# Three real products a complex one in the columns of an inverse transform, with weight preparation moved to GpSimd and its DMAs

## The chip, the cores and the metric

The kernel runs on one core of a Trainium2 chip. The metric is the device time of one execution in microseconds (us); the median of several runs is given. A core has TensorE (PE in the profile; its weight loads are PEld), VectorE (DVE), ScalarE (ACT), GpSimd (POOL), and SyncE (SP), which here only issues DMAs. Each engine works through its own instructions in order and waits on semaphores for the others. DMAs are issued from SP, ACT and POOL.

## The reference

What is computed is one block of a network on x of 2048 rows and 512 columns, in f32. Six rows of modulation (sa, ca, ga, sb, cb, gb) come from `silu(c) @ w_mod`. Then:

```python
h = _layernorm(x, axis=-1) * (1 + ca) + sa
x = x + ga * _A_ref(h, A_w_r, A_w_i)   # irfft2(rfft2(h) * (w_r + 1j * w_i))
h = _layernorm(x, axis=-1) * (1 + cb) + sb
x = x + gb * _B_ref(h, B_w1, B_b1, B_w2)   # mish(h @ w1 + b1) @ w2, 1376 wide inside
```

## The kernel before

The kernel has four stages. Stage 1 (the plan `opening`) norms x and does the forward transform: row products, then column products over 128 rows for each of 16 residues n. Stage 2 (the plan `middle`) multiplies by the spectral weights in 17 groups of columns; `store_d` writes its result into two tiles `dd[0]` and `dd[1]`, eight residues n each, in the layout [n, j, c, q]: c is the real part, the imaginary part, and minus the real part; j counts four interleaved columns, q 64 frequencies. Stage 3 finishes the inverse transform: `p3_col(n)` multiplies the complex columns of residue n by a complex matrix, `p3_row(n)` does the inverse along rows with `kiv` and adds to x. Stage 4 is the dense part: `up` products with w1, mish, `down` products with w2, over four pairs of blocks i and five groups t of 256 of the inner width (a sixth, single group is 96 wide).

The products of stage 4 work in a split f32 form: each operand is a high part, rounded to f32r, and a low part, the difference; three products (`TERMS`) stand for one. Most of stage 4 uses seven products of quarter blocks in place of eight, so sums of quarters of w1 and of w2 are prepared too. This preparation runs beside stage 3 and the first pair of stage 4:

- `load_w1(t)` brings a group of w1; `block_w1(t, a)` casts a quarter to its high part on ACT (line 872) and subtracts to get the low part on DVE (line 873); `sum_w1(t, a, step)` forms a sum on DVE (line 893) and later splits it; `keep_w1` writes the split quarters to DRAM, from where `fetch_w1` brings them again for later pairs into a ring of eight tiles `wr`.
- `load_w2(t)` brings a group of w2; `sum_w2` forms four sums on DVE (line 1046); `split_w2` casts on ACT (line 1049) and subtracts on DVE (line 1050).

In stage 3, `p3_col(n)` has for each of four j two products into one region of a bank: real and imaginary columns by `kc[0]` (line 992), imaginary and minus the real ones by `kc[1]` (line 993). A product of f32 operands 128 by 128 shows as two passes in the profile, so a residue has 16 passes there. ACT copies the whole bank out (line 995), `p3_row` makes four products from the copy (line 1002, eight passes), and DVE adds the bank to x and sums its rows (line 1005). `row_squares` then scales the sum on ACT (line 1009) and sums squares on ACT (line 1010).

Nothing but the order of emission schedules the work. Each step is put into a plan with a key; the keys sort the steps, and a list of places written out by hand, `ORDERS`, gives the order in which the sorted steps are emitted, one list for each of three plans (stages 1, 2, and 3 with 4). Since each engine runs in order, this list sets all queues, those of DMA issues too. POOL's queue holds low parts of stage 1, one product of stage 2, some of `store_d`, the issue of `send` and `turn_out` (rows turned through DRAM), and the last accumulation into x.

Of the kernel before, what the change touches and what calls it, by code (L numbers as in the profile page):

```python
# [102 lines left out]
def tile_spectral_block(ctx: ExitStack, tc: tile.TileContext, x_d, w1_d, b1_d, w2_d,  # L103
# [44 lines left out]
    def plain(t):  # L148
        return t.bitcast(F32)
# [19 lines left out]
    mraw = big.tile([P, N2, 256], F32, name="mraw", tag="da")  # L169
    mring = big.tile([P, 8, 2, 384], F32R, name="mring", tag="db")  # L170
    wmc = big.tile([P, 4, 512], F32, name="wmc", tag="cr")
    wms = big.tile([P, 4, 512], F32, name="wms", tag="ci")

    first = ExitStack()
    pw = first.enter_context(tc.tile_pool(name="pw", bufs=1))
# [1463 lines left out]
```

## Time and profile before

| | us |
|---|---|
| median of 3 runs | 368.36 (367.98 to 369.48) |
| span of the profiled execution | 365.9 |
| DVE busy | 302.7 |
| ACT busy | 266.5 |
| POOL busy | 77.5 |

The span goes from the first to the last instruction of one profiled execution; the time of a run is taken outside it, and the median stands 2.5 us above this span. Stage 1 takes the first 50 us or so, stage 2 goes to 89 us, the column products of stage 3 run from 90.4 to 131.4 us, and the first products with w1 begin at 131.8 us. In the views, a line such as L992 is a line of the kernel; "out<-in" names the tiles; "x16" counts instructions. Busy time of an engine that nobody waits for costs nothing, and a busy PE may still be waiting inside, since the ends of its matmuls are modelled; so the starts of its instructions are of more use than its busy share.

### The profile page before, as it was taken

What the parts mean: (1) busy time and instruction counts of PE and PEld (TensorE: products, weight loads), DVE (VectorE), ACT (ScalarE), POOL (GpSimd) and SP (SyncE); (2) the same over time, 40 slices, a digit from 0 to 9 for tenths busy, and PEclk for the clock granted to TensorE, in tenths of its full rate; (3) what the DMA queues carried; (4) which work ended last, traced back from release to release, by engine and by line L of the source; (5) the groups of instructions that cost most, each with busy time, mean ns of one, the idle gap of its engine ahead of it and who ended that gap; (6) DMA issues with size and microseconds to landing.
All of it is one profiled execution on the core that took longest, in us unless ns stands there. A gap on an engine that the chain in (4) does not pass through costs nothing.

```text
span 365.9 us, 7823 instructions
## 1 busy us (share of the span) xinstructions
PE 358.1 (98%) x2676; PEld 334.6 (91%) x2676; DVE 302.7 (83%) x751; ACT 266.5 (73%) x603; POOL 77.5 (21%) x126
## 2 busy tenths in 40 slices
PE   8999999999999999999999999999999999999995
PEld 7999977768999998798999999999999999999994
DVE  0899977879799889989996677997588984779995
ACT  1789879997799999998767577765686654456650
POOL 0488828787011001100002201005001000000000
PEclk9999999999999999999999999999999999999998
DMA  6999997884669869999889985778989567883133
GB/s 223 380 352 331 380 373 254 275 308 149 179 221 294 265 219 299 253 301 307 276 226 316 303 271 116 261 228 212 283 261 284 188 187 232 238 299 60 60 57 116
DMA packets 54343, 89.96 MB, mean 246 GB/s; under 512 B 7552, under 2 KB 20960, under 8 KB 54048
## 3 DMA queue, kind: packets, MB, share of 16 engines
q1 hardware_dynamic: 49728, 74.65, 62.3%
q0 software_dynamic: 2416, 7.87, 9.4%
q10 hardware_dynamic: 2160, 6.95, 5.5%
q8 instruction: 21, 0.34, 0.4%
q14 instruction: 18, 0.15, 0.1%
HBM read 68.21 MB, written 17.57 MB: 234 GB/s over the span
## 4 chain that ended last, share of the span: by engine, by line
PE 85%; DVE 5%; ACT 3%; POOL 2%; issue 1%; DMA 1%; SPq 0%; ACTq 0%; DVEq 0%; POOLq 0%
PE bank L1224 24%; PE bank L1124 22%; PE bank L1107 6%; PE bank L276 4%; PE bank L992 4%; PE bank L1002 4%; PE bank L993 4%; PE bank L324 3%; PE bank L1170 3%; PE bank L1220 3%; PE bank L325 2%; PE bank L326 2%; DMA wmc<-in_w_mod_dram 1%; PE bank L648 1%; PE bank L624 1%
## 5 line engine op out<-in xcount | busy, mean ns | idle before, releaser
L1124 PE MATMUL bank<-hT,wr 128*128 128x256 f32 x360 | 51.8, 283 | 0.0
L1124 PEld LDWEIGHTS bank<-hT,wr 128*128 128x128 f32 x360 | 47.2, 191 | 0.7
L1124 PE MATMUL bank<-hB,wr 128*128 128x256 f32 x318 | 45.4, 284 | 0.0
L1124 PEld LDWEIGHTS bank<-hB,wr 128*128 128x128 f32 x318 | 41.5, 191 | 0.7
L1276 POOL DMA_DIRECT2D x<-modr x7 | 6.3, 898 | 141.3 <-ACT ah L1049 37.8
L1224 PE MATMUL bank<-w2a,ah 128*128 128x256 f32 x161 | 34.8, 283 | 0.0
L1050 DVE TENSOR_TENSOR al<-buf,ah 128x512 fp32r<-128x512 f32 (+1 forms) x45 | 30.0, 670 | 5.0 <-ACT ah L1049 4.9
L1224 PE MATMUL bank<-w2b,ah 128*128 128x256 f32 x147 | 32.2, 283 | 0.0
L1049 ACT CAST ah<-buf 128x512 fp32r<-128x512 f32 (+1 forms) x45 | 26.8, 603 | 4.1 <-PE bank L1224 1.8
L1224 PEld LDWEIGHTS bank<-w2a,ah 128*128 128x128 f32 x161 | 27.0, 192 | 0.3
L1224 PEld LDWEIGHTS bank<-w2b,ah 128*128 128x128 f32 x147 | 25.0, 191 | 0.6
L992 PE MATMUL bank<-kc,d 128*128 128x128 f32 x128 | 24.9, 276 | 0.5 <-ACT d L545 0.5
L993 PE MATMUL bank<-kc,d 128*128 128x128 f32 x128 | 24.8, 275 | 0.0
L1107 PE MATMUL bank<-hB,wr 128*128 128x512 f32 x96 | 23.8, 391 | 0.0
L1224 PE MATMUL bank<-w,ah 128*128 128x256 f32 x112 | 21.5, 284 | 0.0
L1107 PEld LDWEIGHTS bank<-hB,wr 128*128 128x128 f32 x96 | 17.6, 188 | 3.5
L324 PE MATMUL bank<-buf,mring 128*128 128x512 f32 x48 | 20.5, 426 | 0.0
L992 PEld LDWEIGHTS bank<-kc,d 128*128 128x128 f32 x128 | 19.4, 192 | 0.7 <-ACT d L545 0.7
L993 PEld LDWEIGHTS bank<-kc,d 128*128 128x128 f32 x128 | 19.4, 192 | 0.0
L697 PEld LDWEIGHTS bank<-kv,a_sb 128*128 128x128 f32 x126 | 15.6, 192 | 3.4 <-issue 1.4
L1224 PEld LDWEIGHTS bank<-w,ah 128*128 128x128 f32 x112 | 17.6, 191 | 0.4
L921 POOL DMA_DIRECT2D turned<-x x16 | 9.3, 662 | 40.9 <-DVE buf L1194 22.4
(308 smaller groups left out, 1097.5 us busy)
## 6 DMA issues: line engine op xcount, KB each, us to landing
wr<-w_S SPq DMA_DIRECT2D x60, 256.0 KB, 3.7
wr<-w_A SPq DMA_DIRECT2D x45, 256.0 KB, 3.8
w_S<-hT SPq DMA_DIRECT2D x20, 256.0 KB, 3.0
x<-in_A_x_dram SPq DMA_DIRECT2D x16, 256.0 KB, 4.7
xring<-in_x_t_dram SPq DMA_DIRECT2D x16, 256.0 KB, 4.8
w_A<-wr SPq DMA_DIRECT2D x15, 256.0 KB, 3.9
x<-modr POOLq DMA_DIRECT2D x7, 512.0 KB, 5.4
out_dram<-x SPq DMA_DIRECT2D x7, 512.0 KB, 3.3
```

Source lines behind the costliest of these rows:

```text
L276: nc.tensor.matmul(pgv[:, j], data(j), krs[:, j, :].rearrange("p (c q) -> p c q", c=2), start=True, stop=True)
L324: nc.tensor.matmul(pa, m[:, a, 0:128], g, start=(i == 0), stop=False)
L697: nc.tensor.matmul(pd[:, i * P:(i + 1) * P], y[:, i * P:(i + 1) * P], kv[:, 0:128], start=True, stop=True)
L992: nc.tensor.matmul(o, dj[:, 0:128], kc[0][:, n, :], start=True, stop=False)
L993: nc.tensor.matmul(o, dj[:, 64:192], kc[1][:, n, :], start=False, stop=True)
L1002: nc.tensor.matmul(px[:, j * P:(j + 1) * P], e[:, j * P:(j + 1) * P], kiv[:, j, :], start=True, stop=True)
L1049: nc.scalar.copy(h, r)
L1050: nc.vector.tensor_tensor(l, r, plain(h), op=ALU.subtract)
L1107: nc.tensor.matmul(ups[i, t, f], ring[t, a][:, p, b, :], sides[int(a[2]) - 1][:, :, q, b, :], start=(a[2] == "1" and b == 0 and n == 0), s ...
L1124: nc.tensor.matmul(o, w[:, p, k, :], h[:, q, k, :], start=(first and n == 0), stop=(last and n == 5), skip_group_check=True)
L1170: nc.tensor.matmul(ups[i, 0][:FL], w1s[:, p, u, :], sides[u // 2][:, :, q, u % 2, :], start=(u == 0 and p + q == 0), stop=(u == 3 and p == ...
L1224: nc.tensor.matmul(out_ps[b][n][:, 256 * half:256 * half + 256], a[p][:, e], w2[t][q][:, r], start=(t == 1 and half == 0 and i == 0), stop ...
```

## The change

Let a column be R + iI and the matrix C + iS, as `kc` now holds them in three planes: C, S - C and -C - S. The old form took RC - IS and RS + IC by four real products. The new one takes (R + I)C, then R(S - C) and I(-C - S): the first plus the second is the imaginary part, the first plus the third the real part. `dd` gets the layout [c, n, j, q], with R + I in the third place of c, where minus R was. A residue's steps are now:

- `p3_col`: R by S - C into the first half of a bank, R + I by C into the second, two matmuls of 128 columns each (eight passes);
- `p3_copy`: ACT copies the second half out to `g2`;
- `p3_imag`: two DVE adds of bank and copy, 64 partitions each, into the imaginary half of `e`;
- `p3_last`: I by -C - S, added to the second half in the bank (four passes), from the new tiles `kch`;
- `p3_real`: two ACT copies, 64 partitions each, into the real half of `e`;
- `p3_row` as before, one residue later; banks alternate between tags A and D.

`store_d` forms R + I with an addition on DVE or POOL after the copy, in place of the scaling by -1 on ACT, DVE or POOL. The tiles `kch` (1 MB) are loaded from SP's queue in stage 2 and lie in the pool `act`, whose two buffers later hold `acts`; that pool is opened at the start now, and `acts` is one tile of both parts.

The weights: the high parts of the quarters of w1, and of the raw blocks of w2, come straight from DRAM by DMAs issued from POOL that write f32r (`high_w1`, `high_w2`); the casts on ACT for these are gone. Low parts of quarters of w1, for groups 1 and 2, and of w2, for groups 1 to 3, and the sums of the same groups, are formed on POOL and not on DVE. The casts and low parts of the sums of w1 stay on ACT and DVE. The scaling in `row_squares` goes from ACT to POOL. `single_w1` takes `wsum` and not `g2` for its raw block.

The order lists of the second and third plan are new; that of the first is the same. In stage 2 the new list differs in the last third, from about the eleventh group on. In the third plan all steps move: `p3_col` runs two to three residues ahead of `p3_row`, columns 5 and 4, and 9 and 8, change places, `row_squares` of residues 7 to 15 go behind the last columns, `high_w1` stands several steps before its `block_w1`, and the first `up` products come in between the last column steps, before `p3_last` 13.

```diff
-    dd = [big.tile([P, 8, 4, 3, NQ], F32, name=f"d{i}", tag=t) for i, t in enumerate(("da", "db"))]
+    dd = [big.tile([P, 3, 8, 4, NQ], F32, name=f"d{i}", tag=t) for i, t in enumerate(("da", "db"))]
...
-        elif kind == "all":
-            nc.scalar.mul(minus, s[:, :, 0, :], -1.0)
-        elif kind != "pool" and i:
-            nc.vector.tensor_scalar(minus, s[:, :, 0, :], -1.0, None, op0=ALU.mult)
+        elif kind == "all" or kind != "pool" and i:
+            nc.vector.tensor_tensor(both, s[:, 1], dst[:, 0, :, q0:q0 + nq], op=ALU.add)
         else:
-            nc.gpsimd.tensor_scalar(minus, dst[:, :, 0, q0:q0 + nq], -1.0, None, op0=ALU.mult)
+            nc.gpsimd.tensor_tensor(both, dst[:, 0, :, q0:q0 + nq], dst[:, 1, :, q0:q0 + nq], op=ALU.add)
...
+    def load_kch(i):
+        nc.sync.dma_start(kch[i], kc_d[:, 2, N2 // 2 * i:N2 // 2 * i + N2 // 2, :])
...
+    def high_w1(t, a):
+        slot_w1((t, a))
+        nc.gpsimd.dma_start(ring[t, a][:, 0], w1_block(t, a))
+
     def block_w1(t, a):
-        slot_w1((t, a))
-        split_w1(ring[t, a], w1_block(t, a, src[t]))
+        w = ring[t, a]
+        (nc.gpsimd if t < 3 else nc.vector).tensor_tensor(w[:, 1], w1_block(t, a, src[t]), plain(w[:, 0]), op=ALU.subtract)
...
-            nc.vector.tensor_tensor(v, p, q, op=op)
+            (nc.gpsimd if t < 3 else nc.vector).tensor_tensor(v, p, q, op=op)
...
     def p3_col(n):
-        d = dd[n // 8][:, n % 8]
-        pe = bank("A")
-        for j in range(4):
-            dj = d[:, j].rearrange("p c q -> p (c q)")
-            o = pe[:, j * P:(j + 1) * P]
-            nc.tensor.matmul(o, dj[:, 0:128], kc[0][:, n, :], start=True, stop=False)
-            nc.tensor.matmul(o, dj[:, 64:192], kc[1][:, n, :], start=False, stop=True)
-        e = buf("g1")
-        nc.scalar.copy(e, pe)
-        st["e", n] = e
+        d = dd[n // 8][:, :, n % 8].rearrange("p c j q -> p c (j q)")
+        st["pe", n] = pe = bank("AD"[n % 2])
+        for i, (c, k) in enumerate(((0, kc[1]), (2, kc[0]))):
+            for a in range(2):
+                o = pe[:, (2 * i + a) * P:(2 * i + a + 1) * P]
+                nc.tensor.matmul(o, d[:, c, P * a:P * a + P], k[:, n, :], start=(i == 0 and a == 0), stop=True,
+                                 skip_group_check=True)
+
+    def p3_copy(n):
+        st["s", n] = s = buf("g2")[:, 0:2 * P]
+        nc.scalar.copy(s, st["pe", n][:, 2 * P:])
...
+    def p3_imag(n):
+        st["e", n] = e = buf("g1")
+        to = e.rearrange("p (a b s) -> p b a s", a=2, b=2)
+        for b, (pe, s) in enumerate(zip(halves_of(st["pe", n][:, 0:2 * P]), halves_of(st.pop(("s", n))))):
+            nc.vector.tensor_tensor(to[IM, b], pe, s, op=ALU.add)
+
+    def p3_last(n):
...
+            nc.tensor.matmul(pe[:, (2 + a) * P:(3 + a) * P], d[:, 1, P * a:P * a + P], kch[n // 8][:, n % 8, :],
+                             start=False, stop=True, skip_group_check=True)
+
+    def p3_real(n, b):
+        to = st["e", n].rearrange("p (a b s) -> p b a s", a=2, b=2)
+        nc.scalar.copy(to[RE, b], halves_of(st["pe", n][:, 2 * P:])[b])
...
-        nc.scalar.mul(mv[:, n, 0:1], mv[:, n, 0:1], -D ** -1.5)
+        nc.gpsimd.tensor_scalar(mv[:, n, 0:1], mv[:, n, 0:1], -D ** -1.5, None, op0=ALU.mult)
...
-            nc.vector.tensor_tensor(tsum[:, o], a, b, op=ALU.subtract)
+            (nc.gpsimd if t < 4 else nc.vector).tensor_tensor(tsum[:, o], a, b, op=ALU.subtract)
+
+    def high_w2(t):
+        h = w2[t][0].rearrange("p e d -> p (e d)")
+        for e, f, rows in tiles(t):
+            nc.gpsimd.dma_start(h[:, 256 * e:256 + 512 * e], w2_d[f * P:f * P + rows, 0:256 + 256 * e])
+
+    def split(h, l, r, low=None, high=True):
+        if high:
+            nc.scalar.copy(h, r)
+        (low or nc.vector).tensor_tensor(l, r, plain(h), op=ALU.subtract)
...
+        low = nc.gpsimd if 0 < t < 4 else None
...
-            split(h[:, 768:], l[:, 768:], tsum.rearrange("p e d -> p (e d)"))
+            split(h[:, 768:], l[:, 768:], tsum.rearrange("p e d -> p (e d)"), low)
         else:
             u, v = st["w2", t]
-            split(h[:, 0:256], l[:, 0:256], u[:, 0:256])
-            split(h[:, 256:768], l[:, 256:768], v)
+            split(h[:, 0:256], l[:, 0:256], u[:, 0:256], low, False)
+            split(h[:, 256:768], l[:, 256:768], v, low, False)
...
-        plan.at(1.5 if last else n - N2 + 1.1, p3_row, n)
-        plan.at(1.6 if last else n - N2 + 1.3, row_squares, n)
+        plan.at(n - N2 + 0.2, p3_copy, n)
+        plan.at(n - N2 + 0.3, p3_imag, n)
+        plan.at(n - N2 + 1.02, p3_last, n)
+        for b in range(2):
+            plan.at(n - N2 + 1.04, p3_real, n, b)
+        plan.at(1.5 if last else n - N2 + 2.1, p3_row, n)
+        plan.at(1.6 if last else n - N2 + 2.3, row_squares, n)
...
-    kc = np.stack([z.real, -z.imag], 1)
+    kc = np.stack([z.real, z.imag - z.real, -z.real - z.imag], 1)
```

More of the change, by code (lines that the diff above doesn't have):

```diff
@@ L172, in tile_spectral_block @@
     wms = big.tile([P, 4, 512], F32, name="wms", tag="ci")
+    act = ctx.enter_context(tc.tile_pool(name="act", bufs=2))
+    kch = [act.tile([P, N2 // 2, P], F32, name="kch", tag="act") for _ in range(2)]
     first = ExitStack()
@@ L531, in tile_spectral_block @@
         opening.run(0)
-    dd = [big.tile([P, 8, 4, 3, NQ], F32, name=f"d{i}", tag=t) for i, t in enumerate(("da", "db"))]
+    dd = [big.tile([P, 3, 8, 4, NQ], F32, name=f"d{i}", tag=t) for i, t in enumerate(("da", "db"))]
     def store_d(g, i, part, kind):
         q0, nq = groups[g]
-        src = st["pd", g][:, 0:nq * 128].rearrange("p (q a c) -> p a c q", q=nq, c=2)
-        dst = dd[i].rearrange("p n d c q -> p (n d) c q")
-        s = src[:, 32 * i:32 * i + 32]
-        to, minus = dst[:, :, 0:2, q0:q0 + nq], dst[:, :, 2, q0:q0 + nq]
+        src = st["pd", g][:, 0:nq * 128].rearrange("p (q a c) -> p c a q", q=nq, c=2)
+        dst = dd[i].rearrange("p c n d q -> p c (n d) q")
+        s = src[:, :, 32 * i:32 * i + 32]
+        to, both = dst[:, 0:2, :, q0:q0 + nq], dst[:, 2, :, q0:q0 + nq]
         if part == 0:
@@ L826, in tile_spectral_block @@
             put(load_kc, s - 11)
+            put(load_kch, s - 11)
     with tc.manual_schedule():
@@ L901, in single_w1 @@
         if load:
-            src[0] = buf("g2")[:, 0:4 * FL].rearrange("p (k f) -> p k f", k=4)
+            src[0] = wsum[:, 0:4 * FL].rearrange("p (k f) -> p k f", k=4)
             nc.sync.dma_start(src[0], w1v[:, :, (NF - 1) * P:F])
@@ L1198, in halves @@
         if k == 0:
-            acts[b, t] = [act.tile([P, 7, P], F32R, name=n) for n in ("ah", "al")]
+            both = act.tile([P, 2, 7, P], F32R, name="act", tag="act")
+            acts[b, t] = [both[:, k] for k in range(2)]
         if k < len(parts[b, t]):
@@ L1326, in tile_spectral_block @@
             plan.at(s - N2 + 0.6, fn, *[a for a in args if a is not None])
+            if fn is load_w2:
+                plan.at(s - N2 + 0.7, high_w2, t)
     plan.at(13.6 - N2, load_w2, 0)
@@ L1354, in tile_spectral_block @@
         for a, key in zip(QUARTERS, keys):
+            plan.at(key - 1, high_w1, t, a)
             plan.at(key, block_w1, t, a)
@@ L1462, in tile_spectral_block @@
     plan.at(12, load_w2, 4)
+    plan.at(12.1, high_w2, 4)
+    plan.at(19.1, high_w2, 5)
     plan.at(17, sum_w2, 4, 0, 1, 2, 3)
```

9 lines of the change are left out of this document (5 added, 4 removed), and 134 rows, old and new, of the table ORDERS.

## The prediction

> **What bounds the kernel now.** I read four views in this order: the page's busy times, the engines' shares of the chain that ended last, the busy times by stage, and that chain in order of time.
>
> ```profile
> span 365.9 us, 7823 instructions
> ...
> PE 358.1 (98%) x2676; PEld 334.6 (91%) x2676; DVE 302.7 (83%) x751; ACT 266.5 (73%) x603; POOL 77.5 (21%) x126
> ...
> PE 85%; DVE 5%; ACT 3%; POOL 2%; issue 1%; DMA 1%; SPq 0%; ACTq 0%; DVEq 0%; POOLq 0%
> ```
>
> TensorE is busy 98% of the span and carries 85% of the chain. A modelled busy time could hide gaps, so the next two views look at the stage that changes (columns: time, then busy us and count of PE, PEld, DVE, ACT, POOL, then the granted clock, DMA share, GB/s; in the chain: start, length, what).
>
> ```profile
> 70.00:90.00 20.00, 19.06 (x120) 14.39 (x118) 16.99 (x35) 17.64 (x44) 16.86 (x24) 1.00 0.72 255
> ...
> 90.00:100.00 10.00, 9.62 (x85) 9.62 (x86) 7.84 (x23) 7.02 (x19) 0.00 (x0) 1.00 0.56 175
> 100.00:132.00 32.00, 32.00 (x289) 32.00 (x288) 29.19 (x84) 31.58 (x84) 2.43 (x4) 1.00 0.80 252
> 132.00:180.00 48.00, 48.00 (x301) 43.07 (x300) 45.73 (x119) 43.97 (x105) 2.16 (x4) 1.00 0.89 281
> 180.00:220.00 40.00, 40.00 (x320) 38.99 (x319) 30.37 (x79) 27.80 (x56) 5.35 (x9) 1.00 0.88 276
> ```
>
> ```profile
> 102.35 0.89 PE bank L1002 x8
> 103.24 0.22 PE bank L992 x2
> 103.47 0.22 PE bank L993 x2
> ...
> 105.03 0.89 PE bank L1002 x8
> ...
> 131.83 0.72 PE bank L1124 x6
> ...
> 145.52 4.78 PE bank L1107 x21
> ```
>
> One column of stage 3 starts every 2.68 us (102.35 to 105.03), and the chain is PE alone: 16 passes of 0.11 us for the column products (L992, L993) and 8 for the row products (L1002, 0.89 us). 24 passes in 2.68 us are 0.1115 us each, with no gap. So TensorE's issue sets the time here. But the margin is thin: from 100 to 132 ACT is busy 31.58 of 32 us and DVE 29.19, from 132 to 180 DVE 45.73 of 48 and ACT 43.97. Only POOL is free, 0.00 to 2.43 us a window. From 180 on DVE has a quarter free (30.37 of 40).
>
> **The change, part by part.** *Products.* L992 and L993 issue 128 passes each, 16 a column; six products instead of eight leave 12.
>
> ```profile
> L992 PE MATMUL bank<-kc,d 128*128 128x128 f32 x128 | 24.9, 276 | 0.5 <-ACT d L545 0.5
> L993 PE MATMUL bank<-kc,d 128*128 128x128 f32 x128 | 24.8, 275 | 0.0
> ```
>
> 64 passes by 0.1115 us are **7.1 us less** TensorE work, all on the chain. That is the whole gain; everything else can only keep it or give it back.
>
> *What the three products cost ACT and DVE.*
>
> ```profile
> L995 ACT COPY buf<-bank 128x512 f32<-128x512 f32 x16 | 9.2, 572 | 1.9 <-PE bank L993 1.9
> L545 ACT COPY d<-bank 128x256 f32<-128x256 f32 x5 | 1.8, 376 | 0.5 <-PE bank L697 0.5
> L1009 ACT ACTIVATE mv<-mv 128x1 f32<-128x1 f32 x16 | 3.2, 200 | 0.4 <-DVE x L1005 0.4
> L872 ACT CAST wr<-hT 128x256 fp32r<-128x256 f32 x20 | 7.7, 404 | 0.7 <-DMA hT<-in_B_w_dram 0.7
> L1149 DVE TENSOR_TENSOR even<-even,bank 128x256 f32<-128x256 f32 x1 | 0.4, 422 | 0.0
> L873 DVE TENSOR_TENSOR wr<-hT,wr 128x256 fp32r<-128x256 f32 x20 | 8.2, 420 | 0.0
> L1050 DVE TENSOR_TENSOR w2a<-modr,w2a 128x1024 fp32r<-128x1024 f32 x1 | 1.2, 1222 | 0.0
> L1049 ACT CAST w2b<-wide 128x512 fp32r<-128x512 f32 x1 | 0.6, 622 | 0.3 <-DMA wide<-in_B_w_dram 0.3
> L1050 DVE TENSOR_TENSOR w2b<-wide,w2c 128x512 fp32r<-128x512 f32 x1 | 0.7, 689 | 0.0
> ```
>
> ACT's one copy of 512 elements (0.572) becomes one of 256 and two of 256 on half the partitions; the nearest row is L545, 0.376 each, so 16 x (3 x 0.376 - 0.572) = +8.9 us. ACT loses the 16 small scalings of `row_squares` (L1009, -3.2), 20 casts of `block_w1` (L872, 0.404, -8.1) and the raw casts of `split_w2` for five groups, 256 and 512 elements (about 0.40 + 0.62, -5.1). Net -7.5. DVE gains two adds of 256 from PSUM a column (L1149, 0.422, 32 x 0.422 = +13.5) and loses 8 low parts and 8 sums of w1 and 12 sums of w2 at 0.42 (-11.8), and the w2 low parts of groups 1 to 3 (256, 512 and, for two of them, 1024 elements: 3 x (0.42 + 0.69) + 2 x 1.22 = -5.8). Net -4.1. From 90 to 180 ACT was busy 7.02 + 31.58 + 43.97 = 82.6 us and DVE 82.8; that becomes 75.1 and 78.7 in 90 - 7.1 = 82.9 us. So by their own work both still fit, ACT with 7.8 us over and DVE with **4.2 us**. I cost the work itself at nothing, hidden behind PE; without that spare each further us on DVE is a us of the kernel.
>
> *What POOL takes on.*
>
> ```profile
> L266 POOL TENSOR_TENSOR mring<-mraw,mring 128x256 fp32r<-128x256 f32 x16 | 11.7, 735 | 12.4 <-ACT mring L262 12.4
> L313 POOL TENSOR_TENSOR buf<-wide,buf 128x512 fp32r<-128x512 f32 x7 | 9.0, 1284 | 5.3 <-ACT buf L307 3.6 <-ACT wide L305 1.7
> L551 POOL TENSOR_SCALAR d<-d 128x128 f32<-128x128 f32 x13 | 6.8, 532 | 0.7 <-ACT d L545 0.7
> L938 POOL DMA_DIRECT2D turned<-wide x6 | 3.5, 587 | 57.1 <-DMA wide<-in_B_w_dram 31.1 <-DVE wide L931 25.8 <-DVE hT L873 0.2
> ```
>
> Up to the last `p3_row` of the new order, POOL has 31 operations on 256 elements (0.735), 3 on 512 (1.284) and 2 on 1024 (2.38 if the step from 256 to 512 goes on): 31.4 us; 21 DMA issues at 0.587 (L938): 12.3; small scalings about 3. Together 46.9 us. TensorE's list up to the same place is 16 x 20 x 0.1115 + 8 x 0.72 + 3 x 0.68 = 43.5 us (L1124's six passes 0.72; L1107's three 4.78 / 7). POOL is as full as PE, but its last 4.9 us there are `sum_w2` and `split_w2` of group 3, wanted only by a much later `down`. Cost nothing, if nothing holds POOL up.
>
> *What POOL and DVE do to each other.* The trace has one case of a DVE operation with both inputs in SBUF while POOL reads SBUF:
>
> ```profile
> 44.32 1.20 DVE L195 SCALAR_TENSOR_TENSOR bank<-wms,scb 128x512 f32<-128x512 f32 x1
> ...
> 44.21 0.75 POOL L266 TENSOR_TENSOR mring<-mraw,mring 128x256 fp32r<-128x256 f32 x1
> ...
> L195 DVE SCALAR_TENSOR_TENSOR wm<-wm,bank 128x512 f32<-128x512 f32 x7 | 4.6, 681 | 0.0
> ```
>
> The same operation with its second input in PSUM takes 0.681; here it takes 1.20, 0.52 more, about as long as POOL still had to run. Stage 1 and 2 hardly show it, since their DVE work reads a bank. In the new stage 3 the DVE adds and `p3_row` read a bank too, but 24 larger operations up to the last `p3_row` read SBUF twice (10 low parts and 3 sums of w1, 4 of `split_in`, 4 `gate_sum`, 3 others; 12.5 us). POOL's tensor work fills 31.4 of 43.5 us, 72%. A DVE operation that meets one waits half of 0.735: 24 x 0.72 x 0.37 = 6.4 us. The ends are 0 (they never meet) and 24 x 0.52 = 12.5. I take 6.4, the mean; 4.2 of it is DVE's spare, so **2.2 us** reach PE.
>
> The Trainium skill, "SBUF — State Buffer", Who interferes with whom, has this as a rule: a VectorE instruction with two SBUF inputs and a GpSimd one that reads SBUF share a read interface, and the later one blocks fully. By that rule the trace agrees (0.52 us), and it speaks against this change.
>
> *High parts by POOL's DMAs and kch.* 20 blocks of 128 KB, five of 384 KB, and 1 MB of kch are 5.6 MB more.
>
> ```profile
> turned<-x POOLq DMA_DIRECT2D x16, 128.0 KB, 4.1
> turned<-wide POOLq DMA_DIRECT2D x6, 256.0 KB, 3.5
> ```
>
> POOL's DMAs land 3.5 to 4.1 us after issue here. Spare transfer time from 90 to 180 is 0.44 x 10 + 0.20 x 32 + 0.11 x 48 = 16 us, at 281 / 0.89 = 316 GB/s some 5.1 MB; 7.1 us less leaves 2.9 for the 4.6 MB that fall there. The overhang of 1.7 MB is 5.4 us of transfers. Ends: 0 and 5.4. I take 0, since in the new order other steps of its engine stand between almost every `high_w1` and its `block_w1`, and the fetches go on into a stretch where DVE and ACT are loose. The two `load_kch` go on SP's queue behind `load_kc`, 15 us before use; nothing of SP's waits for them.
>
> *Stage 2 and the seam.* `both` is an addition after the copy where `minus` was a scaling. 13 of POOL's go from 0.532 to at most 0.735 (2.6 us, where POOL has 3.1 of 20 free from 70 to 90): nothing. At the seam PE waits 0.5 us for the last copy (L992's row); the addition comes after it, but four passes of `p3_col` (0.45 us) need only the copy, which covers an add of 128. Zero, at most 0.3.
>
> **The sum.** The profiled execution: 365.9 - 7.1 + 2.2 = 361.0 us of span. Its span lies 2.5 us under the median of the runs, 368.36, and I keep that distance: **363.4 us**.
>
> **The rivals.** *Full cover.* The order keeps POOL and DVE apart, PE never waits: 368.4 - 7.1 = 361.2. For it: PE from 100 to 220 has no idle time even with ACT at 99%. Against: POOL at 72% leaves little room to avoid meetings. *DMA becomes the limit.* High parts land late, DVE and POOL wait in order, `p3_real` and `p3_row` queue behind: 368.4 - 7.1 + 5.4 = 366.7; for it the shares of 0.80 to 0.89, against it 1.67 MB of the overhang may simply fall behind 180. *POOL becomes the bound (slower).* If every one of the 12.5 us meets POOL and POOL is the one that waits, POOL needs 46.9 + 12.5 = 59.4 us for the first part; without the 4.9 that can be late, 54.5 against 43.5. ACT's casts in `sum_w1` wait for POOL's sums, and behind them in ACT's queue stand `p3_real` and `p3_copy`, for which PE waits. 368.4 - 7.1 + 11.0 = 372.3. It decides as soon as POOL falls 8.9 us behind. For it: POOL's list is as long as PE's, and sums feed casts at once (`sum_w1 2 S2`). Against: four fifths of the worst case must come true, and the meetings split between DVE and POOL.
>
> **How the numbers follow.** A measurement of this kernel can tell about 0.5%, 1.8 us, from no change. Forecast (362.3 to 364.6) 0.36; full cover (361.0 to 362.3) 0.24; a part of the DMA or lock ends (364.6 to 366.5) 0.13; DMA limit (366.5 to 370.2) 0.12; POOL bound (over 370.2) 0.15. Faster 0.73, same 0.12, slower 0.15. The range 361.0 to 369.0 leaves out the POOL bound and a third of the one before, about 0.19.
>
> **What would show it.** Right: 192 column passes at 0.11 us; columns about 2.23 us apart; DVE operations of 256 elements with two SBUF inputs longer than 0.42 us wherever POOL's run; PE idle between 90 and 180 of about 2 us. Wrong: PE waiting for POOL's tiles or for landings (the other rivals), DVE lengths unchanged beside POOL (no lock), or POOL's 256-element operation far from 0.735.

## The result, and the profile after

The changed kernel is **slower**: 396.67 us median of 4 runs (394.28 to 397.62) against 368.45 for the kernel before on the same chip (367.98 to 369.48); the ratio is 1.0748, with a 95% interval of 1.0709 to 1.0788. The profiled execution has a span of 395.8 us, 29.9 more than before.

The page of the kernel after, its busy times and its shares of the chain that ended last:

```profile
span 395.8 us, 7816 instructions
...
PE 363.8 (92%) x2612; PEld 333.7 (84%) x2612; DVE 313.5 (79%) x759; ACT 265.7 (67%) x580; POOL 136.2 (34%) x208
...
PE 61%; DVE 12%; DMA 9%; ACT 6%; POOL 6%; issue 3%; SPq 1%; ACTq 1%; DVEq 0%; POOLq 0%
```

TensorE has its 64 instructions less (2612 for 2676), yet it is busy 5.7 us longer and idle 32.0 us of the span (395.8 - 363.8) where it was 7.8. Its share of the chain fell from 85% to 61%. The busy time of ScalarE is nearly the same (266.5 before), that of VectorE is 10.8 us more. Busy time counts a moment once, though operations in a dense row overlap a little at their ends. Added up one by one, the lengths of ScalarE's operations in the trace fell from 306.6 to 299.0 us, and those of VectorE's rose from 346.5 to 353.9.

The busy times by stage of the kernel after, in stretches that the prediction used (time, then busy us and count of PE, PEld, DVE, ACT, POOL, then granted clock, DMA share, GB/s):

```profile
90.00:100.00 10.00, 8.38 (x67) 7.55 (x65) 7.95 (x24) 4.91 (x14) 5.39 (x9) 1.00 0.42 120
100.00:132.00 32.00, 26.55 (x210) 24.41 (x208) 28.62 (x71) 22.07 (x59) 26.86 (x41) 1.00 0.79 220
132.00:180.00 48.00, 38.13 (x206) 33.08 (x207) 35.84 (x82) 34.21 (x78) 31.85 (x42) 0.86 0.83 243
180.00:220.00 40.00, 32.77 (x227) 29.29 (x225) 32.67 (x80) 29.48 (x61) 2.80 (x4) 1.00 0.86 264
```

The loss lies between 90 and 220. TensorE did 301 instructions from 132 to 180 before, now 206. ScalarE, which was full from 100 to 132 (31.58 us), has 22.07 there. GpSimd alone does more there (26.86 us for 2.43), and it is not full either, so no engine is the new bound by its own work. The DMA share is no higher than before on the mean (0.80 and 0.89 before), so bandwidth does not bound the whole stretch. It is uneven, though: 0.95 from 120 to 130 and 0.94 from 130 to 140, around TensorE's longest wait, where the kernel before had 0.81 and 0.71. For these 20 us a bound by transfers is not excluded.

The chain of waits of the kernel after, in order of time (start, length, what):

```profile
94.95 0.91 PE bank L1006 x8
95.85 0.27 issue
96.12 0.76 POOL w L1086
96.88 6.69 DMA w<-in_B_w_dram
103.64 1.26 POOL w L1091
...
130.88 4.44 DMA wr<-in_B_w_dram
135.42 0.42 issue
135.83 0.58 ACT wide L972
136.43 0.37 ACT buf L1011
136.80 0.26 ACT buf L1031
137.07 0.38 ACT buf L1031
137.50 2.07 PE bank L1006 x8
```

Before, this view had TensorE alone. Now it runs for most of 100 us over GpSimd, landings of high parts (L1086, L887) and of turned rows, and VectorE, and touches TensorE only for a few passes. The reader is to see how one late landing spreads: ScalarE's scaling of turned rows (L972) starts only at 135.83, the copies of a column (L1011, L1031) stand behind it in ScalarE's order, and TensorE's next column waits for them. The chain names a high part as what landed last before L972; what L972 reads are the turned rows, so the landing that it needed may be theirs.

What TensorE waited for between 88 and 215 (engine, tile and line, releaser, us in total, times, longest), the longest four:

```profile
PE bank L1006 <- ACT buf L1031: 6.4, 1, 6.4
PE bank L1026 <- DVE buf L1020: 3.4, 4, 1.2
PE bank L1149 <- DMA wr<-in_B_w_dram: 3.3, 2, 1.7
PE bank L1037 <- ACT buf L1031: 2.5, 2, 2.2
```

No single wait carries the loss. It is many, in both stages, with different releasers.

### The profile page after: what moved, and what is told of

It is laid out like the page before. It is cut to its first block, busy times and chain, and to the rows that moved or that the text cites. A ratio compares the mean times of both kernels' runs of the same rounds, so it can differ in the third digit from the quotient of the medians.

```text
span 395.8 us, 7816 instructions
## 1 busy us (share of the span) xinstructions
PE 363.8 (92%) x2612; PEld 333.7 (84%) x2612; DVE 313.5 (79%) x759; ACT 265.7 (67%) x580; POOL 136.2 (34%) x208
## 4 chain that ended last, share of the span: by engine, by line
PE 61%; DVE 12%; DMA 9%; ACT 6%; POOL 6%; issue 3%; SPq 1%; ACTq 1%; DVEq 0%; POOLq 0%
PE bank L1267 20%; PE bank L1166 20%; PE bank L285 4%; PE bank L333 3%; PE bank L1263 2%; DMA wr<-in_B_w_dram 2%; PE bank L1212 2%; DMA wide<-turned 2%; DMA w<-in_B_w_dram 2%; DMA turned<-wide 1%; PE bank L334 1%; PE bank L335 1%; DMA wr<-w_A 1%; PE bank L346 1%; DVE wide L204 1%
## 5 line engine op out<-in xcount | busy, mean ns | idle before, releaser
L1267 PE MATMUL bank<-w2a,act 128*128 128x256 f32 x217 | 38.0, 283 | 0.0
L1267 PE MATMUL bank<-w2b,act 128*128 128x256 f32 x196 | 34.6, 284 | 0.0
L1091 DVE TENSOR_TENSOR act<-buf,act 128x512 fp32r<-128x512 f32 (+1 forms) x45 | 30.0, 669 | 4.2 <-ACT act L1090 4.0
L1267 PEld LDWEIGHTS bank<-w2a,act 128*128 128x128 f32 x217 | 31.9, 191 | 0.6
L1090 ACT CAST act<-buf 128x512 fp32r<-128x512 f32 (+1 forms) x45 | 26.8, 603 | 4.5 <-PE bank L1267 2.4
L1267 PEld LDWEIGHTS bank<-w2b,act 128*128 128x128 f32 x196 | 29.0, 191 | 0.8 <-DVE act L1091 0.2
L1149 PEld LDWEIGHTS bank<-hB,wr 128*128 128x128 f32 x96 | 18.0, 199 | 11.4 <-DVE wr L891 3.1
L1267 PE MATMUL bank<-w,act 128*128 128x256 f32 x168 | 25.7, 286 | 0.0
L972 ACT ACTIVATE wide<-wide,cols 128x256 f32<-128x256 f32 x28 | 15.1, 594 | 14.4 <-DMA wide<-turned 8.0
L1006 PE MATMUL bank<-kc,d 128*128 128x128 f32 x128 | 17.7, 286 | 6.8 <-ACT buf L1031 6.4
L1267 PEld LDWEIGHTS bank<-w,act 128*128 128x128 f32 x168 | 22.9, 192 | 0.9 <-DVE act L1091 0.2
L1267 PE MATMUL bank<-w2hi,act 128*128 128x256 f32 x98 | 21.5, 285 | 1.0 <-ACT act L1090 0.5
L1006 PEld LDWEIGHTS bank<-kc,d 128*128 128x128 f32 x128 | 16.2, 200 | 7.2 <-ACT buf L1031 6.6
L1037 PE MATMUL bank<-kiv,buf 128*128 128x128 f32 x128 | 18.9, 298 | 2.5 <-ACT buf L1031 2.5
```

Source lines behind the costliest of these rows:

```text
L972: nc.scalar.activation(o, o, AF.Identity, bias=cols[:, 1, 0, k:k + 1], scale=cols[:, 1, 1, k:k + 1])
L1006: nc.tensor.matmul(o, d[:, c, P * a:P * a + P], k[:, n, :], start=(i == 0 and a == 0), stop=True, skip_group_check=True)
L1037: nc.tensor.matmul(px[:, j * P:(j + 1) * P], e[:, j * P:(j + 1) * P], kiv[:, j, :], start=True, stop=True)
L1090: nc.scalar.copy(h, r)
L1091: (low or nc.vector).tensor_tensor(l, r, plain(h), op=ALU.subtract)
L1149: nc.tensor.matmul(ups[i, t, f], ring[t, a][:, p, b, :], sides[int(a[2]) - 1][:, :, q, b, :], start=(a[2] == "1" and b == 0 and n == 0), s ...
```

## The experiments

Two rounds of theories came first and a third after they fell. The early ones: (1) GpSimd's tensor work, by its own length or by holding up VectorE; (2) the high parts by DMA; (3) the longer way of a column (product, copy, adds, last product, copies, row: two more hand-overs there and back than before) or the new order. Unless said otherwise, a time is one run beside one run of the kernel before on the same chip, and the difference to that run is what is read. The runs of before lay between 367.6 and 369.0, so differences under 1.5 us are not read. The four runs of the kernel after spread by 3.3 us, so between slowed kernels even 3 us is little.

### Undoing parts of the change

`e1_sums_dve`: sums and low parts back on VectorE, in the new order.

```diff
-        (nc.gpsimd if t < 3 else nc.vector).tensor_tensor(w[:, 1], ...
+        nc.vector.tensor_tensor(w[:, 1], ...
-            (nc.gpsimd if t < 3 else nc.vector).tensor_tensor(v, p, q, op=op)
+            nc.vector.tensor_tensor(v, p, q, op=op)
-        low = nc.gpsimd if 0 < t < 4 else None
+        low = None
```

> The changed kernel with the sums and low parts of weights back on DVE; high parts still by POOL's DMAs, order of steps as changed. Theory 1 (POOL's tensor work, its late queue and the shared read port make the loss): most of it goes, the time is set by DVE's extra 17.6 us over its spare, about 374 (370 to 380), and the DVE operations longer than usual beside POOL (8.6 us of excess after the change) are gone. Theory 2 (high parts landing late and their DMAs make the loss): only the lock's 9 us come back at best, 386 to 400. Theory 3 (the new order and the longer chain of a column make it): 385 or more.

`e2_high_act`: high parts cast by ScalarE again, no DMAs for them.

```diff
-        nc.gpsimd.dma_start(ring[t, a][:, 0], w1_block(t, a))
...
+        nc.scalar.copy(w[:, 0], w1_block(t, a, src[t]))
...
-            nc.gpsimd.dma_start(h[:, 256 * e:256 + 512 * e], w2_d[f * P:f * P + rows, 0:256 + 256 * e])
```

> The changed kernel with the high parts cast on ACT again, as part of block_w1 and split_w2; no high_w1 or high_w2 DMA, sums and low parts still on POOL, order as changed. Theory 2 (late landings and DMA load): ACT has 13 us more work, but the loss mostly goes: 368 to 376. Theory 1 (POOL's tensor work and the port): POOL loses only 12 to 20 us of issues, 383 to 395. Theory 3 (order and column chain): 388 or more.

`e3_three_only`: both edits together, so that three products in the new order are left.

> The changed kernel with both undone: sums, low and high parts as before on DVE and ACT; what remains is the three products, the new order and the scaling of row_squares on POOL. Theories 1 or 2: DVE then has about 96 us of work and ACT 88 where PE has 83, so 374 to 380. Theory 3 (the new order and the column chain cost it): 388 or more.

`e4_old_sums_pool`: the kernel before in its own order, with sums and low parts of the same groups on GpSimd.

```diff
-            nc.vector.tensor_tensor(v, p, q, op=op)
+            (nc.gpsimd if t < 3 else nc.vector).tensor_tensor(v, p, q, op=op)
```

> The kernel before, in its own order, with sums and low parts of the same groups on POOL (w1 of groups 1 and 2, w2 of groups 1 to 3), no other edit. Theory 1 (POOL's tensor work, in-order queue and port): the sends of turned rows queue behind 31 us of POOL work, and DVE is held at the port; 375 to 390. Theories 2 and 3: POOL's work alone is harmless where DVE loses as much as it waits, 367 to 371.

Measured, with before at 368.92: e1 400.33, e2 387.82, e3 396.0, e4 369.88. In the old order GpSimd's tensor work costs 1.0 us. In the new one it gains 8.2 us without the DMAs (396.0 to 387.8), and beside them 3.2 us, which is near what can be read (31.4 to 28.2 over before). Theory 1 falls. The high parts by DMA cost about 9 us (28.2 over before with them, 18.9 without), and 4.3 where VectorE has the sums. Theory 2 holds for that much. About 19 us were left.

The lock between VectorE and GpSimd, which the prediction took from one case, is there all the same. The pages' first rows of e4, and of e1 beside the one of after above:

```profile
PE 359.3 (98%) x2676; PEld 335.3 (91%) x2676; DVE 294.1 (80%) x715; ACT 266.7 (72%) x603; POOL 109.3 (30%) x162
```

```profile
PE 364.9 (92%) x2612; PEld 334.0 (84%) x2612; DVE 320.5 (80%) x795; ACT 265.1 (67%) x580; POOL 102.3 (26%) x172
```

Both moves take 36 operations from VectorE (751 to 715, 795 to 759), by the prediction's lengths 17.6 us, but its busy time falls by only 8.6 (302.7 to 294.1) and 7.0 (320.5 to 313.5). Of what is missing, 2 to 3 us are overlaps that busy time had not counted in the first place. By their own lengths, added up, the operations fell by 11.4 us (346.5 to 335.0) and 9.0 (362.9 to 353.9). So 6.2 us in e4 and 8.6 in the kernel after went into longer operations, for example this one of the kernel after, 417 ns before:

```profile
L883 DVE TENSOR_TENSOR hT<-hT,hT 128x256 fp32r<-128x256 f32 x16 | 9.3, 582 | 2.7 <-ACT hT L882 2.5
```

In the kernel after, VectorE's rounding subtractions of 256 elements with both inputs in SBUF took 706 ns on the mean where a tensor operation of GpSimd ran at the same time (9 of them) and 420 ns where none did (25). Its adds that read a bank (L1020) took 423 ns either way (22 and 10).

### A column of three products in the old order

`e5_old_order_pool`, `e6_old_order_dve`: the order lists of before, where only a column's steps are rewritten; casts by ScalarE; sums on GpSimd or on VectorE.

```diff
+        if name == "p3_col":
+            out = [(p3_col, (n,)), (p3_copy, (n,))]
+            if n:
+                out += [(p3_last, (n - 1,)), (p3_real, (n - 1, 0)), (p3_real, (n - 1, 1))]
+            if n > 1:
+                out += [(p3_row, (n - 2,))]
+            return out + [(p3_imag, (n,))]
```

> The order of before, with only the steps of a column rewritten for three products (at the old place of column n: column n, the copy of n, last and real of n-1, row of n-2, imag of n); sums and low parts of the same groups on GpSimd, high parts cast by ScalarE. Theory order (the new order of steps makes the loss): about 365 to 372 us, since ScalarE then has some 91 of 83 us of work between 90 and 173 and becomes the bound by part of it. Theory chain (a column's longer chain copy, imag, last, real, row makes the loss in any order): 380 us or more, with PE idle of 20 us or more between 90 and 210.

> As the run before it, but sums and low parts on VectorE: three products alone in the old order. Theory order: about 372 to 378 us, since VectorE gains 13.5 us of adds between 90 and 173 and has no spare for them. Theory chain: 380 us or more. If GpSimd's tensor work were harmful in itself, this one would be faster than the run before it.

`e7_old_stage2`: the kernel after with the old list for stage 2 alone.

> The changed kernel with the order of stage 2 of before (kch loaded directly behind kc). If stage 2's new order and the kch loads cost the 3.4 us by which the first column starts later: about 393 us and a first column near 90.4. If the addition for the third product costs them: 396 to 397 as before.

Measured, with before at 368.81: e5 392.03, e6 394.18, e7 395.4. With casts by ScalarE, three products are about as slow in the old order as in the new one (e5 beside e2, e6 beside e3), and 22 us slower than four (e5 beside e4). e7 leaves 1.6 us at most to stage 2. The rows of e5 by stage:

```profile
100.00:132.00 32.00, 19.34 (x143) 18.24 (x143) 23.69 (x53) 24.99 (x71) 21.16 (x26) 0.94 0.52 163
132.00:180.00 48.00, 40.75 (x250) 36.67 (x250) 37.60 (x96) 41.52 (x106) 7.56 (x11) 0.93 0.61 191
180.00:220.00 40.00, 40.00 (x296) 38.17 (x295) 37.13 (x97) 31.83 (x69) 0.91 (x1) 1.00 0.88 274
```

Here the whole loss lies in the columns; stage 4 after 180 has no idle time. This looked like the column's chain, so its hand-overs were loosened.

`e8_imag_first`, `e9_imag_first_banks`, `e10_lag`, `e11_lag_balanced`: in e5's order, the adds ahead of the row; the halves of a column in banks of their own; every step a place later than the one that it waits for; and some of ScalarE's work given away. Steps that need a row's statistics move back as far as the rows do.

```diff
+        out += [(p3_imag, (n - 1,))]
+        out += [(p3_last, (n - 2,)), (p3_real, (n - 2, 0)), (p3_real, (n - 2, 1))]
+        out += [(p3_row, (n - 3,))]
...
-        st["e", n] = e = buf("g1")
+        st["e", n] = e = st["es"][n % 3]
```

> As e5_old_order_pool (392.0), but the adds of column n stand ahead of the row of column n-2 in the order (at the place of column n: column n, copy n, imag n, last and real of n-1, row n-2), which needs a third buffer for the row's input, taken from the other ring. In e5 the records show a closed loop: the row of n-2 (0.9 us of passes), VectorE's add of it (0.77), the two adds of the imaginary part (0.86), the last passes (0.45), the next row: some 3.3 us with the hand-overs, where TensorE's own work is 2.23. Theory loop: the loop is cut and the time falls to 366 to 374, what is left being ScalarE's 8.9 us more work. Theory chain (four hand-overs more a column on engines that work in order, whatever the order of the list): 385 or more.

> As the run before it, with the two halves of a column in banks of their own (A and D), so that the last passes wait only for the copy of their own half and not for VectorE's adds on the other. If that wait by banks costs time: faster than the run before it by 2 us or more. If the adds are done by then anyway: the same within 1 us, or slower, since two columns are in flight and not four.

> As e8_imag_first, with every step of a column one place later than the one that it waits for (column n, copy n, imag n-1, last and real n-2, row n-3). If the queues' hand-overs make the loss, the slack of a whole place takes it away: 366 to 372, and faster than e8 by 3 us or more. If the work itself on ScalarE is the limit: the same as e8 within 2 us.

> As e10_lag, with the small scalings on GpSimd (ScalarE 3.2 us less) and one of the four real copies of each pair of columns on VectorE (ScalarE 3.0 us less, VectorE about 3 more). If ScalarE's work is the limit in e10: 4 to 6 us faster than it. If hand-overs are: the same within 2 us.

Measured, with before at 369.0: 400.16, 398.97, 406.0, 413.8. Banks of their own bring 1.2 us (e8 to e9), which is within what can be read; for the rest the expectations failed, in one direction: each loosening made it slower. The chain of e10 shows what a list written without a view of the other queues does:

```profile
107.40 0.71 DVE x L1096 x2
...
108.37 0.82 ACT bank L1101 x2
...
109.21 0.30 ACT rstd L211
...
109.78 0.17 DVE ve L219
...
110.52 0.60 DVE wide L199 x2
...
111.16 0.28 DVE buf L1076
```

VectorE adds a row (L1096), ScalarE waits for it to take its squares (L1101) and the logarithm (L211), VectorE waits for that (L219), and the adds of the next column (L1076) stand behind in VectorE's order. A short chain of tiny operations on two engines in order stops both, and TensorE with them: it waits 24.1 us for these adds, in 12 times.

### Cutting the column's hand-overs

`e12_sends_sync`: the kernel after, the stores of turned rows on SyncE's queue.

```diff
-        nc.gpsimd.dma_start(turned[n - n % 2][at:at + P], ...
+        nc.sync.dma_start(turned[n - n % 2][at:at + P], ...
```

> The changed kernel with the stores of the turned near rows on SyncE's queue instead of GpSimd's. In the changed kernel TensorE stands 6.5 us at 130.6, behind a chain real copy, scalings of the turned rows, reload, stores issued at 119.8 to 126.9 (105.6 before), and its next passes run at half speed for another 2.9 us. Theory queue (the stores stand in GpSimd's order behind its sums and issues): that gap goes, 385 to 390 us, as much as casting the high parts on ScalarE gave (387.8). Theory hand-over: the gap moves elsewhere and the time stays above 393.

`e13_cut_last`, `e14_cut_row`, `e15_cut_both`: e2's kernel, where the adds read another bank, the rows a constant tile, or both.

```diff
-        for b, (pe, s) in enumerate(zip(halves_of(st["pe", n][:, 0:2 * P]), ...
+        for b, (pe, s) in enumerate(zip(halves_of(scp[:, 0:2 * P]), ...
...
         e = st.pop(("e", n))
+        e = flat2(kiv)
```

> The kernel of e2_high_act (387.8), with VectorE's adds of the imaginary part reading another bank in place of the column's, so that the last passes no longer wait for them; as many operations of the same size (the imaginary parts are wrong). Theory hand-over by the bank: TensorE waited 5.7 us ahead of the last passes in e2; 378 to 383. If the order is so tied that the wait moves to the next link: 385 or more.

> The kernel of e2_high_act, with the passes of a row reading a constant tile in place of the column's result, so that they wait neither for the copies nor for the adds; all operations are kept (the rows are wrong). TensorE waited 3.1 us ahead of the rows in e2: 382 to 386 if only that goes; under 378 if the whole round trip is the cause.

> Both cuts. The passes of stage 3 then wait only for the evictions that free their banks. Theory hand-over (the two new round trips of a column make most of the loss): 365 to 375 us. Theory work or order (ScalarE's and VectorE's own operations, or the order in stage 4): 380 or more, with TensorE idle 20 us or more between 90 and 210.

Measured, with before at 368.52: e12 399.67, e13 390.36, e14 388.31, e15 390.02. With no hand-over left between the adds, the last products and the rows, e2's kernel is as slow as with them (18.9 us over before; e15 21.5). In this order these hand-overs are not the cause, though TensorE did wait for them by name. e12 is not faster, but it doesn't settle its theory: on SyncE's queue the stores came no earlier. They were issued from 119.7 to 133.4 (119.8 to 126.9 in the kernel after, from 105.6 on before), and TensorE's wait ahead of L1006 is 5.1 us where it was 6.4. Late turned rows stay a rival.

### The order by itself, and the gain by itself

`e16_new_order_four`: e2's kernel with the old column in the new order, and four buffers for the input of a row.

```diff
+        for i in range(2):
+            for a in range(2):
+                o = pe[:, (2 * i + a) * P:(2 * i + a + 1) * P]
+                nc.tensor.matmul(o, d[:, i, P * a:P * a + P], kc[0][:, n, :], start=True, stop=False)
+                nc.tensor.matmul(o, d[:, 1 - i, P * a:P * a + P], kc[1][:, n, :], start=False, stop=True)
...
+        nc.scalar.copy(e, st.pop(("pe", n)))
```

> The kernel of e2_high_act (387.8) with the column of before in the new order: eight products in one step, one copy of 512 elements by ScalarE, no adds, no last passes, no real copies (rows come out in another arrangement and are wrong). TensorE has 7.1 us more, VectorE 13.5 less, ScalarE 8.9 less. Theory order (the new order of the steps idles the engines whatever the column is): 380 us or more. Theory column (three products cost the engines more than they save, in hand-overs or work): 368 to 374, as the old order with the sums on GpSimd (369.9).

`e17_old_order_cut`: e5's kernel with the two cuts of e15.

> The kernel of e5_old_order_pool (392.0: three products in the old order) with both hand-overs of a column cut as in e15. In e5 TensorE idles 30 us in stage 3 and nothing after 160. Theory column in this order: the stage runs free, 364 to 372. Theory order: 380 or more.

`e18_before_fewer`: the kernel before with two products of a column left out and nothing else.

```diff
-            nc.tensor.matmul(o, dj[:, 0:128], kc[0][:, n, :], start=True, stop=False)
-            nc.tensor.matmul(o, dj[:, 64:192], kc[1][:, n, :], start=False, stop=True)
+            nc.tensor.matmul(o, dj[:, 0:128], kc[0][:, n, :], start=True, stop=j > 1)
+            if j < 2:
+                nc.tensor.matmul(o, dj[:, 64:192], kc[1][:, n, :], start=False, stop=True)
```

> The kernel before with two of the eight products of each column left out (64 passes of 0.1115 us less, as three products a complex one would save, but with the old copy and no adds; half of each result lacks a product). Theory TensorE bound: 368.4 - 7.1 = 361.3 us. Theory three engines bound (ScalarE has 0.13 to 0.16 us free in every 10 between 100 and 130, VectorE is as full around 115 and from 140 on): 365 to 368, with TensorE idle 4 us or more between 90 and 180 where before has 0.2.

Measured: e16 387.32 and e17 386.72, with before at 367.61; e18 365.93 (10 runs, 365.33 to 369.28) against 368.23 (13 runs), a ratio of 0.9948, interval 0.9924 to 0.9972.

**e16** is 19.7 us over before with the column of before, where the old order with GpSimd's sums had 1.0 (e4). So the new list costs 18.7 us (19.7 - 1.0) even with that column; with it go the additions of `store_d`, the loads of kch and the small scalings on GpSimd, which were not taken apart further. Its busy times, its rows by stage, and then e4's row for the columns:

```profile
PE 367.9 (95%) x2676; PEld 339.9 (88%) x2676; DVE 300.5 (78%) x727; ACT 266.9 (69%) x578; POOL 114.8 (30%) x178
```

```profile
100.00:132.00 32.00, 32.00 (x289) 32.00 (x288) 19.87 (x48) 20.29 (x49) 18.76 (x28) 1.00 0.57 191
132.00:180.00 48.00, 40.87 (x218) 34.26 (x217) 39.61 (x90) 40.92 (x96) 20.30 (x27) 0.93 0.71 224
```

```profile
100.00:132.00 32.00, 30.36 (x264) 29.68 (x264) 22.89 (x54) 28.18 (x75) 23.21 (x28) 1.00 0.67 206
```

VectorE and ScalarE have about as much work in all as before (302.7 and 266.5). From 100 to 132 TensorE runs its columns without a gap, as before, but ScalarE and VectorE do 20 us of work there instead of 31.58 and 29.19. e4 has the same sums on GpSimd, so it is the fairer neighbour: beside it, most of what is missing is ScalarE's (20.29 for 28.18 us, 49 operations for 75), while VectorE has lost 3 us. The longest waits of the two for TensorE, between 88 and 215:

```profile
ACT buf L1013 <- PE bank L1007: 7.9, 5, 3.5
```

```profile
DVE x L1031 <- PE bank L1028: 5.8, 6, 2.2
```

In the new list the column's steps stand ahead of other work on these engines, so they wait for TensorE's columns with that work behind them undone. Of the 7.9 us that e16's ScalarE does less than e4's in this stretch, some 2 are weight preparation and some 4 belong to the turned rows: two of their scalings (L972) for eight, and no split for one. Stores of turned rows are issued from 120.2 on in e16, from 106.0 on in e4. After 132 stage 4 needs that work, and TensorE waits in turn: it is busy 40.87 of 48 us and does 218 instructions where it did 301. Its longest wait between 88 and 215 is for the split of the turned rows, and VectorE makes that split late because it waits for them to land:

```profile
PE bank L1157 <- DVE hB L998: 3.0, 2, 2.3
```

```profile
DVE hB L998 <- DMA even<-turned: 4.4, 1, 4.4
```

These are a few us of the 18.7; that late turned rows cause the rest is not shown.

**e18** is the ceiling in the order of before: 64 passes less, with nothing given for them, are worth 2.3 us (1.0 to 2.8 by the interval) and not 7.1. Its row for the columns, and TensorE's wait:

```profile
100.00:132.00 32.00, 29.38 (x250) 28.22 (x249) 28.89 (x84) 31.58 (x85) 2.43 (x4) 1.00 0.81 256
```

```profile
PE bank L1003 <- ACT buf L996: 3.2, 5, 1.4
```

ScalarE is busy 31.58 of 32 us, the same as before to the digit; TensorE now waits for its copies. In this order stage 3 was bound by ScalarE as much as by TensorE. The wait of 3.2 us is two thirds of the 4.8 that are missing; where the rest went was not followed. e17 points the same way: its hand-overs are cut, its loss stays in the columns, and TensorE waits there for ScalarE's copy 16.3 us in 12 times. The three products gave ScalarE some 8.5 us more to do (L1029 and L1049 of e5, below, for L995's 9.2) in a stretch that had none free before. But e17's ScalarE is busy 27.80 of 32 us from 100 to 132, so its work alone doesn't explain the wait; whether the place of the copies in its order has a part was not tested.

```profile
L1049 ACT COPY buf<-bank 64x256 f32<-64x256 f32 x32 | 11.7, 367 | 5.6 <-PE bank L1044 5.1
L1029 ACT COPY buf<-bank 128x256 f32<-128x256 f32 x16 | 6.0, 372 | 0.8 <-PE bank L1024 0.5
```

No version that computes everything beat the kernel before.

## Why the prediction was wrong

The forecast was 363.4 us, the range 361.0 to 369.0; the time was 396.7. The step that failed is "I cost the work itself at nothing, hidden behind PE", which rests on TensorE as the only bound: the gain of 7.1 us was taken in full, and the new order, the longer way of a column and the high parts by DMA had no price. The pieces, as differences to the run of before on the same chip: sums and low parts on GpSimd +1.0 (e4); the new order and what goes with it +18.7 (e4 to e16); three products for four in that order -0.8 (e16 to e2); high parts by DMA +9.3 (e2 to after). The sum is 28.2, what was measured (the first and third pieces are too small to be told from nothing); it follows one path, and in another order of edits the shares differ. GpSimd's sums gain 8.2 inside the new order. And three products cost 22.3 us when they come first, in the old order (e4 to e5), where the new order then gives 4.3 back (e5 to e2). So the new order and the three products cost about 20 us each when put in alone, and together no more than that; the runs don't divide it between them.

- **"TensorE's issue sets the time here."** This is where it failed first. The passes were counted rightly (128 and 64 column passes in the profile after), but the view that proves TensorE full, starts without gaps, doesn't prove it alone. The row with ACT at 31.58 of 32 was quoted and called a thin margin; in the rivals "no idle time even with ACT at 99%" was even taken for the change. It was a second bound: of 7.1 us e18 could keep 2.3. Neither e16 to e2 (0.8 us) nor e4 to e5 (22.3 us lost) shows the 7.1.
- **The new order had no term in the sum.** It was described, and costed only through single steps. On the path above it is the largest piece, 18.7 us. "By their own work both still fit" adds busy times as if engines in order could pack them; e16 has hardly more work than before on ScalarE or VectorE and still leaves both idle for over a third of the columns' time (e4 left VectorE idle for 28% of it and ScalarE for 12%).
- **High parts "0 (ends 0 and 5.4)".** Both ends were worked out from transfer rates; the measured piece is 9.3 us. The DMA share rose over e2's, which has no such loads (rows of e2 below, beside 0.79 and 0.83), though not on the mean over that of before. The traces also show longer landings: the first high part took 6.69 us (96.88 in the chain), where a cast of 512 elements on ScalarE took 0.62, and others got longer with it. The rival "DMA becomes the limit" had this way of the loss, late high parts that hold engines in order, and priced it at 5.4 us. First e2's rows by stage, then the stores and reloads of turned rows between 88 and 160 (KB each, median us to landing) of the kernel after and of e2:

```profile
100.00:132.00 32.00, 28.65 (x228) 26.63 (x228) 28.89 (x71) 28.23 (x76) 19.27 (x30) 1.00 0.61 205
132.00:180.00 48.00, 39.97 (x221) 33.83 (x222) 42.91 (x98) 41.52 (x99) 18.98 (x26) 0.96 0.70 226
```

```profile
turned<-even POOLq DMA_DIRECT2D x2, 256.0 KB, 6.6
wide<-turned SPq DMA_DIRECT2D x4, 128.0 KB, 6.3
```

```profile
turned<-even POOLq DMA_DIRECT2D x2, 256.0 KB, 3.9
wide<-turned SPq DMA_DIRECT2D x4, 128.0 KB, 3.3
```

  That these landings are the cause of the whole 9.3 is argued from the chain; no run changed their length alone.
- **The lock.** The Trainium skill, "SBUF — State Buffer", Who interferes with whom, gave the mechanism, and the runs agree: predicted 6.4 us on VectorE, measured 6.2 (e4) and 8.6 (e1 to after) by the lengths of its operations. The size was about right. That 2.2 us of it reach the end was not borne out: in e4 the whole move costs 1.0, and in the new order it pays.
- **"Net -4.1" on VectorE** missed a second thing: in `store_d` 9 scalings on VectorE became 17 additions of the same size (284 ns) and 4 smaller ones, 3.2 us more, which the part on stage 2 priced for GpSimd alone. With the lock the lengths of its operations rose 7.5 us where the sum had 2.3; that busy time rose by 10.8 is because fewer of them overlap.
- **"Net -7.5" on ScalarE** came out (306.6 to 299.0 by lengths), but by luck: the sum left out 12 scalings of `store_d` that went (3.4 us) and three more ACT_TABLE_LOADs of 1.28 us, seven for four, that every kernel here in the new order has and none in the old one. They come behind 190, where e16's TensorE shows no wait on ScalarE.
- **The rival "POOL becomes the bound"** had the right sign for the wrong reason. GpSimd's list alone is not what costs the time: it is busy 26.86 of 32 us in the columns, and taking its DMAs away helps while taking its sums away hurts.
- **"Stage 2 and the seam: zero, at most 0.3."** The old list there gains 1.6 us at most (e7), near what can be read.

What stays open: which moves in the list make the 18.7 us (the later turned rows are a candidate that no run moved alone), why three products cost as much in the old order, and whether some order of three products would reach e18's 365.9. The rewritings of the old list tried here gave 392 to 414, the new list with casts by ScalarE 387.8.

## What to carry to other kernels

Before pricing work that is taken off the busiest engine, look in that stage for the second busiest: one at 99% is not cover but the next bound, and a version that simply leaves the work out shows in one run what the rest of the stage allows. Where a list sets the order on engines that run in order, a new list is a change by itself and is tested with the old work in it. A wait that has a name in the trace isn't yet a cause: cutting it (e13 to e15) can leave the time where it was.

## What the runs showed that was not expected

TensorE ran slowly after a long pause. In the kernel after, with the wait of 6.4 us at 131, the granted clock (third number from the end) was:

```profile
120.00:130.00 10.00, 9.18 (x77) 8.68 (x76) 9.47 (x24) 7.68 (x20) 8.12 (x15) 1.00 0.95 276
130.00:140.00 10.00, 3.62 (x21) 3.43 (x21) 3.49 (x8) 3.71 (x8) 6.44 (x8) 0.66 0.94 278
138.00:142.00 4.00, 4.00 (x21) 4.00 (x20) 0.69 (x1) 2.55 (x6) 3.08 (x3) 0.50 0.17 41
```

The eight passes behind the pause took 2.07 us (137.50 in the chain above), where the eight at 94.95 took 0.91. So a long stall costs more than its own length. The Trainium skill, "TensorE: Matmul & The Clock Gate", HAM oscillation — how this bites in real kernels, has this as a rule (a pause longer than the activity window puts the array back to half rate), and the trace agrees: the clock granted from 138 to 142 is 0.50, and 2.07 is a little over twice 0.91.

GpSimd's queue moved data at a higher price in engine time when it carried the high parts. By queue between 88 and 160 (packets, MB, share of 16 engines), first before, then after:

```profile
q1 hardware_dynamic: 12523, 15.49, 70.3%
q0 software_dynamic: 640, 2.10, 7.8%
```

```profile
q1 hardware_dynamic: 8615, 10.24, 46.6%
q0 software_dynamic: 4176, 3.67, 21.8%
```

The high parts show in q0 (in e2, without them, it moved 1.31 MB in this stretch). Its packets fell from 3.3 KB to 0.9 KB on the mean (2.10 MB by 640, 3.67 by 4176), and a MB on it took 5.9% of the stretch's engine time instead of 3.7%; on q1 it was 4.5% both times.
